# A linear-attention and SiLU MLP kernel: r and k turned on VectorE from a grouped copy, the product in four row groups, y and r16 turned by DMA, a ramp with half blocks

## The chip, the cores and the metric

The kernel runs on one core of a Trainium2 chip. The metric is the device time of one launch in microseconds (us). Before the change the median of two runs is 228.84 us (228.53 and 229.16). The profile is of one further execution of the same program.

## The reference

For four batches (B), eight heads (H), 768 tokens (S) and a head width D of 48, a decaying state is carried over the tokens, and its output goes through a two-layer MLP with SiLU.

```python
for t in range(S):
    cur = np.einsum('bhd,bhe->bhde', u[None] * kt, vt)
    y[:, :, t] = np.einsum('bhd,bhde->bhe', rt, state + cur)
    state = w[None, :, :, None] * state + np.einsum('bhd,bhe->bhde', kt, vt)
...
x = np.ascontiguousarray(attn_out.transpose(0, 2, 1, 3)).reshape(B * S, H * D)
h = x @ w_in
g = h * (1.0 / (1.0 + np.exp(-h)))
return (g @ w_out).astype(np.float32)
```

All inputs and the output are float32; x is 3072 x 384, w_in 384 x 2048, w_out 2048 x 384.

## The kernel before

The tokens are cut into six chunks of 128 (C). A unit is one chunk of one batch, so there are 24 units; unit i is chunk i // 4 of batch i % 4, and `sc` is the chunk. Each unit works on all eight heads, in four pairs (NP). One list of instructions is written out by hand for each engine: the kernel runs under a manual schedule, so each engine takes its work in the order of the program.

For one unit:

- `load` (L96 to L104) issues three DMAs on SP's queue for r, k and v, four units ahead (NIN is 4). A row of one head is 48 floats, so the pieces are 192 bytes long.
- `p1_natural` casts v to half precision on ScalarE and makes on GpSimd, from the rows as they lie, `ku` = k*u (L145), `rku_f` = r*ku (L147), and `kc`, k with the decay to the end of the chunk (L148). VectorE sums rku_f over a head (L151), and GpSimd makes `vu`, the bonus term (L153).
- `p1` turns r and k with eight TensorE transposes in float32 (L165) into PSUM. VectorE multiplies them by the decay tables into `rT` and `kT` (L167, L169). From chunk 1 on ScalarE casts rT to half precision (L172).
- `p2` multiplies kT by rT per head in float32: `ae` for the even heads in rows 0 to 47 (L179), `ao` for the odd ones in rows 64 to 111 (L181), each into a PSUM bank of its own. VectorE applies the causal mask to both (`am`, L186).
- `p3` adds up y in PSUM from the carried state and from am times v (L198, L201) and makes the new state's part `sps` (L208). VectorE adds vu to y (L211) and updates the state (L221, L224); GpSimd decays the state first (`sdec`, L215) and casts it afterwards (`stb`, L225).
- `p4` turns y with three TensorE transposes (L237), and ScalarE copies it into `xT` (L238), the input of the MLP for the whole chunk.

The MLP of a chunk is a list of 32 fillers. Sixteen are `l1`: three matmuls of 512 columns (L248) and one SiLU on ScalarE (L251). Sixteen are `l2`: four matmuls of 384 columns (L260), and after each fourth of these one eviction on VectorE (L264) and one store on SP (L266). The main loop puts eight fillers into each unit, in groups of two, one, two and three, between the steps of the unit. The four units of a chunk so take up the MLP of the chunk before. Units 0 to 3 have no fillers, and after unit 23 the 32 fillers of the last chunk are left.

The weights come through GpSimd's queue, w_in in three DMAs after unit 0's products (L285), w_out in four after unit 1's product (L292). PSUM is shared out as three banks for `tA` (tr, tk, ae, ao), two for `y` (y, sps, yT) and three for `moe` (hps, ops).

## Time and profile before

| | us |
|---|---|
| median of the runs | 228.84 |
| span of the profiled execution | 226.5 |
| first l1 matmul starts | 42.91 |
| unit 5 to unit 23, from one product to the next | 8.0 each |
| matmuls of the last chunk's MLP, after unit 23 | 20.8 |

| engine | busy us | share of the span |
|---|---|---|
| TensorE matmul | 202.3 | 89% |
| TensorE weight load | 133.1 | 59% |
| VectorE | 115.8 | 51% |
| ScalarE | 94.2 | 42% |
| GpSimd | 119.0 | 53% |

The span runs from the first to the last instruction of the profiled execution; the run's time has about 2.3 us more around it. A busy share is an average over a ramp, a long even stretch and a tail, so the stretches are read one by one. The busy times of two groups of matmuls can overlap, since matmuls are pipelined; the chain of waits counts each moment once.

### The profile page before, as it was taken

To read this page: it belongs to the slowest core of one execution; us is meant where nothing else is said; L and a number is where in the kernel's file an instruction comes from. 1 tells how busy PE (TensorE), PEld (TensorE's weight loads), DVE (VectorE), ACT (ScalarE), POOL (GpSimd) and SP (SyncE) were. 2 spreads that over 40 slices of the span, in tenths; PEclk is the share of its full clock that TensorE was granted. 3 is DMA by queue.
4 is the path that set the end of the run, shared out by engine and by line. 5 is a ranking of instruction groups with operands and counts; after the bars stand their busy time and mean duration, and the time that the engine had idled before them with its cause. 6 is when DMAs were issued, how large, how long until landed. Compare 5 with 4: busy or idle time off the path is not lost.

```text
span 226.5 us, 4378 instructions
## 1 busy us (share of the span) xinstructions
PE 202.3 (89%) x1672; PEld 133.1 (59%) x1672; DVE 115.8 (51%) x225; ACT 94.2 (42%) x173; POOL 119.0 (53%) x150
## 2 busy tenths in 40 slices
PE   1266298799999999999999999999999999999993
PEld 1164177456667656766665776666676557654561
DVE  6157365647368536656833865563685256420020
ACT  2521011586621378411578211866213783029500
POOL 2387975765674665667467466656746561000000
PEclk9999555799999999999999999999999999999999
DMA  5999999992216385026735053923161000110011
GB/s 95 201 196 208 204 185 176 224 186 50 58 38 139 105 177 104 3 76 137 166 77 107 0 142 98 213 48 61 38 142 69 3 0 3 69 53 16 3 69 69
DMA packets 81604, 22.69 MB, mean 100 GB/s; under 512 B 75824, under 2 KB 81200, under 8 KB 81584
## 3 DMA queue, kind: packets, MB, share of 16 engines
q1 hardware_dynamic: 79040, 19.28, 39.3%
q0 software_dynamic: 2544, 3.15, 8.0%
q8 instruction: 13, 0.21, 0.4%
q14 instruction: 7, 0.06, 0.1%
HBM read 20.84 MB, written 4.72 MB: 113 GB/s over the span
## 4 chain that ended last, share of the span: by engine, by line
PE 81%; POOL 8%; DVE 3%; issue 3%; DMA 2%; SPq 1%; DVEq 0%; POOLq 0%
PE hps L248 28%; PE ops L260 28%; PE ae L179 10%; PE tr L165 4%; PE tk L165 4%; PE yT L237 2%; DMA u_bc<-in_u_dram 2%; POOL ku L145 2%; PE y L201 2%; POOL rku_f L147 2%; PE sps L208 2%; PE y L198 2%; POOL wout L292 1%; SPq L102 1%; POOL kc L148 1%
## 5 line engine op out<-in xcount | busy, mean ns | idle before, releaser
L248 PE MATMUL hps<-xT,win 128*128 128x512 f16 x288 | 70.2, 384 | 0.0
L251 ACT ACTIVATE gT<-hps 128x512 f16<-128x512 f32 x96 | 57.4, 598 | 29.5 <-PE hps L248 27.3
L260 PE MATMUL ops<-wout,gT 128*128 128x384 f16 x384 | 69.0, 326 | 0.0
L260 PEld LDWEIGHTS <-gT 128*128 128x128 f16 x384 | 35.8, 98 | 21.2
L248 PEld LDWEIGHTS <-win 128*128 128x128 f16 x288 | 26.7, 99 | 26.5 <-issue 1.3
L186 DVE TENSOR_TENSOR am<-ae,maskM 128x512 f16<-128x512 f32 x24 | 16.6, 691 | 49.1 <-PE ao L181 49.1
L153 POOL TENSOR_TENSOR vu<-vin,rku 128x384 f32<-128x384 f32 x24 | 19.9, 829 | 35.8 <-DVE rku L151 35.8
L179 PE MATMUL ae<-rT,kT 48*128 48x128 f32 x192 | 30.8, 306 | 6.1 <-DVE kT L169 6.1
L179 PEld LDWEIGHTS ae<-rT,kT 48*128 48x128 f32 x192 | 25.8, 206 | 14.2 <-issue 7.5
L264 DVE COPY osb<-ops 128x384 f32<-128x384 f32 x24 | 13.4, 557 | 38.3 <-PE ops L260 37.9
L181 PE MATMUL ao<-rT,kT 48*128 48x128 f32 x192 | 30.8, 306 | 0.0
L238 ACT COPY xT<-yT 128x384 f16<-128x384 f16 x24 | 11.4, 476 | 43.3 <-PE yT L237 43.3
L145 POOL TENSOR_TENSOR ku<-kin,u_bc 128x384 f32<-128x384 f32 x24 | 24.1, 1005 | 7.9 <-DMA u_bc<-in_u_dram 6.7
L172 ACT CAST rT<-rT 112x512 f16<-112x512 f32 x20 | 12.4, 618 | 37.2 <-DVE rT L167 37.2
L181 PEld LDWEIGHTS ao<-rT,kT 48*128 48x128 f32 x192 | 25.8, 206 | 0.0
L147 POOL TENSOR_TENSOR rku_f<-rin,ku 128x384 f32<-128x384 f32 x24 | 24.0, 999 | 1.9
L148 POOL TENSOR_TENSOR kc<-kin,lamC 128x384 f16<-128x384 f32 x24 | 24.0, 999 | 0.8 <-ACT lamC L130 0.8
L225 POOL CAST stb<-st 112x384 f16<-112x384 f32 x20 | 10.1, 503 | 25.0 <-DVE st L221 19.9
L165 PE MATMUL tr<-ident,rin 128*112 128x128 f32 x96 | 16.7, 302 | 5.1 <-DMA rin<-in_r_dram 5.1
L167 DVE TENSOR_TENSOR rT<-tr,lamR 112x512 f32<-112x512 f32 x24 | 16.5, 689 | 4.2 <-PE tr L165 4.2
L151 DVE TENSOR_REDUCE rku<-rku_f 128x8 f32<-128x384 f32 x24 | 13.1, 544 | 10.2 <-POOL rku_f L147 10.1
L165 PEld LDWEIGHTS tr<-ident,rin 128*112 128x112 f32 x96 | 12.5, 147 | 9.0 <-issue 5.9
(46 smaller groups left out, 200.9 us busy)
## 6 DMA issues: line engine op xcount, KB each, us to landing
rin<-in_r_dram SPq DMA_DIRECT2D x24, 192.0 KB, 3.4
kin<-in_k_dram SPq DMA_DIRECT2D x24, 192.0 KB, 3.5
vin<-in_v_dram SPq DMA_DIRECT2D x24, 192.0 KB, 3.6
out_dram<-osb SPq DMA_DIRECT2D x24, 192.0 KB, 1.9
win<-in_moe_w_in_dram POOLq DMA_DIRECT2D x3, 512.0 KB, 8.8
wout<-in_moe_w_out_dram POOLq DMA_DIRECT2D x4, 384.0 KB, 10.3
w_bc<-in_w_dram SPq DMA_DIRECT2D x1, 192.0 KB, 4.3
u_bc<-in_u_dram SPq DMA_DIRECT2D x1, 192.0 KB, 4.1
```

The lines of the kernel that those rows point to most:

```text
L145: nc.gpsimd.tensor_tensor(out=ku, in0=kin[n][:, :, 0:D], in1=u_bc, op=ALU.mult)
L147: nc.gpsimd.tensor_tensor(out=rku_f, in0=rin[n][:, :, 0:D], in1=ku, op=ALU.mult)
L148: nc.gpsimd.tensor_tensor(out=kc[i % 2][:, :, 0:D], in0=kin[n][:, :, 0:D], in1=lamC, op=ALU.mult)
L153: nc.gpsimd.tensor_tensor(out=L["vu"], in0=vin[n], in1=rku.unsqueeze(2).broadcast_to([128, H, D]), op=ALU.mult)
L165: nc.tensor.transpose(t[0:PR, p, :], flat[:, 128 * p:128 * p + PR], ident)
L167: nc.vector.tensor_tensor(out=L["rT"], in0=tr[0:PR], in1=lamR, op=ALU.mult)
L179: nc.tensor.matmul(ae[:, p, :], L["kT"][0:D, p, :], L["rT"][0:D, p, :], start=True, stop=True)
L181: nc.tensor.matmul(ao[:, p, :], L["kT"][64:PR, p, :], L["rT"][64:PR, p, :], start=True, stop=True)
L186: nc.vector.tensor_tensor(out=am, in0=a, in1=maskM.unsqueeze(1).broadcast_to([128, NP, C]), op=ALU.mult)
L248: nc.tensor.matmul(hps, win[q][:, ft * 128:(ft + 1) * 128], xts[sc][:, q, :, :].rearrange("p b t -> p (b t)"), start=(q == 0), stop=(q == ...
L251: nc.scalar.activation(out=gts[sc][:, ft, :], in_=hps, func=AF.Silu)
L260: nc.tensor.matmul(ops, gts[sc][:, ft, b * C:(b + 1) * C], wout[:, ft, :], start=(ft == 0), stop=(ft == NFT - 1))
```

## The change

Units 0 to 3 keep TensorE for turning r, k and y. From unit 4 on:

- Four more DMAs per unit load r and k a second time in grouped form (`ldg`): partition 32*g + j holds four consecutive tokens of head pair g, in pieces of 768 bytes. `decay_g` multiplies them by decay tables in this layout on VectorE, into `rgd` and `kgd`, and `turn_g` turns them with two VectorE block transposes of 32 x 32, straight into SBUF.
- `product_g` does the product for all four head pairs at once in rows 0, 32, 64 and 96: three blocks of 32 rows with 256, 128 and 128 columns each, twelve matmuls in place of eight. Zeros between the two heads in rgd keep them apart.
- The half-precision r for the state comes from a GpSimd multiplication in natural layout (`decayed_r16`), turned by a DMA transpose on SP's queue (`turn_r16`); the ScalarE cast is gone.
- y is turned by a DMA transpose on SP's queue (`turn_y`), straight into xT; the TensorE transposes and the ScalarE copy are gone.
- l2's eviction goes from VectorE to ScalarE, but for the last chunk.

In the ramp, the small loads of w and u go on ScalarE's queue ahead of everything, the weights come in eight pieces spread over units 0 to 3, half of chunk 0's l1 (the first two batches, in matmuls of 256 columns) runs inside units 2 and 3, and the other half comes as eight fillers. PSUM becomes two buffers of two banks (`att`) and four banks (`moe`). Within a unit the fillers come in groups of two, two and four.

```diff
+    def ldg(i, dst, src):
+        sc, b = unit(i)
+        for h in range(2):
+            nc.sync.dma_start(
+                out=dst[i % NIN][:, h].rearrange("p a d -> p (a d)"),
+                in_=bass.AP(tensor=src.tensor, offset=(b * H + h) * S * D + sc * C * D,
+                            ap=[[2 * S * D, NP], [TB * D, TJ], [1, TB * D]]))
+
+    def load(i):
+        if i >= NU:
+            return
+        if i >= B:
+            ldg(i, rg, r)
+            ldg(i, kg, k)
+        ld(i, kin, k, 64)
+        ld(i, rin, r, 64)
+        ld(i, vin, v, D)
...
+    nc.scalar.preload_act_table_set("natural_log_exp_and_others")
+    nc.vector.memset(wpT, 1.0)
+    nc.scalar.dma_start(out=wpT[0:D, :], in_=bass.AP(tensor=w.tensor, offset=0,
+                                                     ap=[[1, D], [PW, NP]]))
+    nc.scalar.dma_start(out=wpT[64:PR, :], in_=bass.AP(tensor=w.tensor, offset=D,
+                                                       ap=[[1, D], [PW, NP]]))
+    nc.scalar.dma_start(out=u_bc, in_=bass.AP(tensor=u.tensor, offset=0,
+                                              ap=[[0, 128], [D, H], [1, D]]))
+    nc.scalar.dma_start(out=w_bc, in_=bass.AP(tensor=w.tensor, offset=0,
+                                              ap=[[0, 128], [1, HD]]))
+    nc.scalar.dma_start(out=w_g, in_=bass.AP(tensor=w.tensor, offset=0,
+                                             ap=[[PW, NP], [0, TJ], [1, PW]]))
...
+    def decay_pe(i):
+        for key, src, lam in (("rT", "tr", lamR), ("kT", "tk", lamK)):
+            L(i)[key] = wrk.tile([PR, NP, C], FP, name=key)
+            nc.vector.tensor_tensor(out=L(i)[key], in0=L(i)[src][0:PR], in1=lam, op=ALU.mult)
+
+    def product_pe(i):
+        a = L(i)["a"] = ps.tile([128, 2, NP, C], FP, name="a", tag="att", bufs=2)
+        rT, kT = L(i)["rT"], L(i)["kT"]
         for p in range(NP):
-            nc.tensor.matmul(ae[:, p, :], L["kT"][0:D, p, :], L["rT"][0:D, p, :],
-                             start=True, stop=True)
-            nc.tensor.matmul(ao[:, p, :], L["kT"][64:PR, p, :], L["rT"][64:PR, p, :],
-                             start=True, stop=True)
-        L["am"] = []
-        for a in (ae, ao):
-            am = wrk.tile([128, NP, C], F16, name="am", bufs=4)
-            nc.vector.tensor_tensor(out=am, in0=a,
-                                    in1=maskM.unsqueeze(1).broadcast_to([128, NP, C]),
-                                    op=ALU.mult)
-            L["am"].append(am)
-
-    def p3(i):
-        sc, b = unit(i)
-        L = live[i]
-        v16 = L["v16"]
-        y = ps.tile([128, H, D], FP, tag="y", bufs=2)
+            for j, r0 in ((0, 0), (1, 64)):
+                nc.tensor.matmul(a[:, j, p, :], kT[r0:r0 + D, p, :], rT[r0:r0 + D, p, :],
+                                 start=True, stop=True)
+
+    def decay_g(i):
+        n = i % NIN
+        d = L(i)["rgd"] = rgd[i % 2]
+        nc.vector.tensor_tensor(
+            out=bass.AP(tensor=d.tensor, offset=d.offset,
+                        ap=[d.ap[0], [H1, 2], [128, TB], [1, D]]),
+            in0=rg[n], in1=lamRG, op=ALU.mult)
+        kd = L(i)["kgd"] = wrk.tile([128, TB, 2, D], FP, name="kgd")
+        nc.vector.tensor_tensor(out=kd.rearrange("p a h d -> p h a d"), in0=kg[n],
+                                in1=lamKG, op=ALU.mult)
+
+    def decayed_r16(i):
+        nc.gpsimd.tensor_tensor(out=r16[i % 2][:, :, 0:D], in0=rin[i % NIN][:, :, 0:D],
+                                in1=lamRn, op=ALU.mult)
+
+    def turn_r16(i):
+        L(i)["rT16"] = wrk.tile([128, NP, C], F16, name="rT16")
+        nc.sync.dma_start_transpose(out=L(i)["rT16"],
+                                    in_=r16[i % 2].rearrange("p h d -> p (h d)"))
+
+    def turn_g(i):
+        rT = L(i)["rT"] = wrk.tile([128, 4, C], FP, name="rTg")
+        kT = L(i)["kT"] = wrk.tile([128, 3, C], FP, name="kTg")
+        nc.vector.transpose(
+            out=kT.rearrange("p b (j a) -> p a b j", a=TB),
+            in_=L(i)["kgd"].rearrange("p a h d -> p a (h d)").rearrange("p a (b j) -> p a b j", j=TJ))
+        nc.vector.transpose(
+            out=rT.rearrange("p b (j a) -> p a b j", a=TB),
+            in_=L(i)["rgd"].rearrange("p a (b j) -> p a b j", j=TJ))
+
+    def product_g(i):
+        a = L(i)["ag"] = [ps.tile([128, 2, 512], FP, name="ag", tag="att", bufs=2) for _ in range(2)]
+        rT, kT = L(i)["rT"], L(i)["kT"]
+        for blk, r0, n, c0 in ((1, 1, 2, 0), (0, 0, 1, 0), (2, 3, 1, 128)):
+            for g in range(NP):
+                rows = slice(TJ * g, TJ * g + TJ)
+                nc.tensor.matmul(a[g // 2][:, g % 2, c0:c0 + 128 * n],
+                                 kT[rows, blk, :],
+                                 rT[rows, r0:r0 + n, :].rearrange("p b t -> p (b t)"),
+                                 start=(blk == 1), stop=(blk != 1), skip_group_check=True)
...
+        ys = L(i)["ys"] = ps.tile([128, 2, 512], FP, name="ys", tag="att", bufs=2)
+        y = ys[:, 0, 0:HD].rearrange("p (h d) -> p h d", h=H)
...
+    def turn_y(i, by_pe):
+        sc, b = unit(i)
+        yf = L(i)["y16"].rearrange("p h d -> p (h d)")
+        x = x_tile(sc)
+        if not by_pe:
+            nc.sync.dma_start_transpose(out=x[:, :, b, :], in_=yf)
+            return
...
+        m = B // nb
+        hps = ps.tile([128, m, nb * C], FP, name="hps", tag="moe", bufs=4)
+        for f in range(m):
+            for q in range(NQ):
+                nc.tensor.matmul(hps[:, f, :], win[:, q, (ft + f) * 128:(ft + f + 1) * 128],
+                                 xts[sc][:, q, b0:b0 + nb, :].rearrange("p b t -> p (b t)"),
+                                 start=(q == 0), stop=(q == NQ - 1))
+        nc.scalar.activation(out=gts[sc][:, ft:ft + m, b0 * C:(b0 + nb) * C], in_=hps, func=AF.Silu)
...
+            if sc < NCH - 1:
+                nc.scalar.copy(out=osb, in_=ops)
+            else:
+                nc.vector.tensor_copy(out=osb, in_=ops)
...
+    def second(sc):
+        return [lambda b=b, p=p: l2(sc, b, p) for b in range(B) for p in range(4)]
+
+    def first(sc):
+        return [lambda f=f: l1(sc, 0, B, f) for f in range(NFT)]
+
+
+    bonus_products(0)
+    ld_win(0)
+    decayed_k(0)
+    turn_pe(0)
+    decay_pe(0)
+    cast_v(0)
+    tables_g()
+    for i in range(2):
+        nc.vector.memset(kc[i][:, :, D:64], 0.0)
+        nc.vector.memset(rgd[i][:, :, D:H1], 0.0)
+        nc.vector.memset(r16[i][:, :, D:64], 0.0)
+    for b in range(B):
+        nc.gpsimd.memset(st[b], 0.0)
+    for i in range(B):
+        product_pe(i)
+        bonus_sum(i)
+        masked(i)
+        bonus_v(i)
+        if i == 0:
+            ld_win(1)
+        if i == 1:
+            ld_win(3)
+        if i == 2:
+            ld_wout(1)
+        if i + 1 < B:
+            bonus_products(i + 1)
+            if i == 0:
+                ld_win(2)
+            if i == 1:
+                ld_wout(0)
+            turn_pe(i + 1)
+        if i == 2:
+            for ft in range(0, NFT // 2, 2):
+                l1(0, 0, 2, ft)
+        if i == 3:
+            for ft in range(NFT // 2, NFT, 2):
+                l1(0, 0, 2, ft)
+        outputs(i)
+        if i + 1 < B:
+            decay_pe(i + 1)
+        evict_y(i)
+        state(i)
+        load(i + NIN)
+        if i + 1 < B:
+            decayed_k(i + 1)
+            cast_v(i + 1)
+        turn_y(i, True)
+        if i == 2:
+            ld_wout(2)
+        if i == 3:
+            ld_wout(3)
+    fillers.extend([lambda ft=ft: l1(0, 2, 2, ft) for ft in range(0, NFT, 2)])
+    fillers.extend(second(0))
+
+    def prepare(i):
+        bonus_products(i)
+        decayed_k(i)
+        decay_g(i)
+        decayed_r16(i)
+        turn_r16(i)
+
+    prepare(B)
+    turn_g(B)
+    cast_v(B)
+    bonus_sum(B)
+    bonus_v(B)
+    decayed_state(B)
+    for i in range(B, NU):
+        sc, b = unit(i)
+        product_g(i)
+        masked(i)
+        if i + 1 < NU:
+            prepare(i + 1)
         fill(2)
-        if i == 1:
-            for g in range(4):
-                nc.gpsimd.dma_start(
-                    out=wout[:, 4 * g:4 * g + 4, :],
-                    in_=moe_w_out[512 * g:512 * g + 512, :]
-                    .rearrange("(f p) n -> p f n", p=128))
+        outputs(i)
+        evict_y(i)
+        state(i)
+        turn_y(i, False)
+        load(i + NIN)
+        fill(2)
         if i + 1 < NU:
-            p1_natural(i + 1)
-            p1(i + 1)
-        load(i + NIN)
-        fill(1)
-        p3(i)
-        fill(2)
-        p4(i)
-        fill(3)
-        sc, b = unit(i)
+            turn_g(i + 1)
+            cast_v(i + 1)
+            bonus_sum(i + 1)
+            bonus_v(i + 1)
+            decayed_state(i + 1)
+        fill(4)
         if b == B - 1:
-            fill(len(fillers))
-            fillers.extend(moe(sc))
+            fillers.extend(first(sc) + second(sc))
```

## The prediction

> **What bounds the kernel now.** I read the page's busy times, then its slices, then the chain of waits over one unit in the even stretch, then the groups of instructions for what the other engines carry. In the slices each digit is tenths of a fortieth of the span (5.7 us); PEclk is TensorE's granted clock and DMA the share of the DMA engines.
>
> ```profile
> PE 202.3 (89%) x1672; PEld 133.1 (59%) x1672; DVE 115.8 (51%) x225; ACT 94.2 (42%) x173; POOL 119.0 (53%) x150
> ...
> PE   1266298799999999999999999999999999999993
> ...
> PEclk9999555799999999999999999999999999999999
> DMA  5999999992216385026735053923161000110011
> ```
>
> The 89% splits in two. In the first eight slices TensorE has gaps, in four of them half its clock, and the DMA engines are full from the second to the ninth. After that TensorE never rests, and DMA averages 0.45 over 76 to 108 us. One unit of that stretch in the chain (start, length, what):
>
> ```profile
> 115.40 0.30 PE ae L179
> ...
> 116.49 1.40 PE hps L248 x6
> 117.89 0.44 PE tr L165 x4
> 118.33 0.44 PE tk L165 x4
> 118.77 0.65 PE hps L248 x3
> ...
> 119.80 0.23 PE sps L208 x4
> 120.02 1.29 PE hps L248 x6
> 121.32 0.17 PE yT L237 x3
> 121.49 1.94 PE hps L248 x9
> 123.43 0.30 PE ae L179
> ```
>
> From ae to ae is 8.03 us, all TensorE: the eight fillers take 5.28 (1.40 + 0.65 + 1.29 + 1.94), the product 1.09 (115.40 to 116.49), the turns of r and k 0.88, that of y 0.17, y and sps 0.61. So a unit's own TensorE work is 2.75. What other engines do costs nothing until one of them needs about 8 us per unit. GpSimd is nearest:
>
> ```profile
> L145 POOL TENSOR_TENSOR ku<-kin,u_bc 128x384 f32<-128x384 f32 x24 | 24.1, 1005 | 7.9 <-DMA u_bc<-in_u_dram 6.7
> L147 POOL TENSOR_TENSOR rku_f<-rin,ku 128x384 f32<-128x384 f32 x24 | 24.0, 999 | 1.9
> L148 POOL TENSOR_TENSOR kc<-kin,lamC 128x384 f16<-128x384 f32 x24 | 24.0, 999 | 0.8 <-ACT lamC L130 0.8
> L153 POOL TENSOR_TENSOR vu<-vin,rku 128x384 f32<-128x384 f32 x24 | 19.9, 829 | 35.8 <-DVE rku L151 35.8
> ```
>
> Mean lengths in ns stand after the busy time. With sdec (0.83) and stb (0.50) GpSimd has 5.16 us of work per unit, and waits for VectorE in the rest.
>
> **What the Trainium skill says.** "TensorE: Matmul & The Clock Gate", in "Why this matters for your kernels", has matmuls of few rows run side by side when they start at partitions 0, 32, 64 and 96: four of them 3.07 times as fast as in turn. The trace before has two such groups: ae and ao start within 10 ns of each other, and a pair of passes takes 0.11 us. Four are not in it. "VectorE: DVE Perf Modes", in "The three transpose paths", gives 311 ns for a 128 x 128 transpose in blocks of 32 on VectorE and 1309 ns on the DMA crossbar, both in half precision; no run here shows either. "SBUF — State Buffer", in "Who interferes with whom", says that a VectorE instruction with two SBUF inputs and a GpSimd instruction that reads SBUF block each other entirely. In the even stretch VectorE's two-input work takes one input from PSUM, so the trace shows no such clash; decay_g will have two SBUF inputs.
>
> **The change, part by part, for units 4 to 23.**
>
> *TensorE.* Turns of r and k go (0.88), and of y (0.17). The product keeps its streaming time if four groups overlap: 256 + 128 + 128 columns are as many as the four pairs of 128 before. But each 0.11 us must then take four weight loads instead of two. Lower bound 1.05 us; upper bound for the theory 1.6; I take 1.2. Own work becomes 2.75 - 0.88 - 0.17 + 0.11 = 1.81, a unit 7.1 us.
>
> *VectorE.* The PSUM multiplications (0.69 + 0.68) and osb (0.56 in half of the units) go. decay_g adds two instructions of 384 elements; as y's addition of that size, 0.56 each (0.5 at least, since no VectorE row of 384 elements is under 0.54; 1.0 if a GpSimd instruction blocks it). turn_g adds transposes of 384 and 512 elements. Their nearest rows are the reduce over 384 (0.54) and the mask over 512 (0.69): 1.25 together; half of that if two elements pass per cycle, 2.5 if four-byte elements take two passes. With masks 1.37, y 0.56, state 0.71 and the reduce 0.54 that is 5.55 us, under 7.1. The loop back to TensorE is longer: product 1.2, handover 0.1, masks 1.37, decay_g 1.1, y 0.56, state 0.71, turn_g 1.25, handover 0.1, so 6.4. It leaves 0.7.
>
> *GpSimd.* decayed_r16 is another kc: 1.0 (0.83 at least). 6.16 us per unit, 0.9 under the period. decay_g lies beside these instructions; blocked, it costs GpSimd up to 1.1 and VectorE a wait of about half an instruction twice. That eats both slacks: 0 to 0.5 us per unit, taken as 0.1.
>
> *SP's queue and DMA.* Per unit SP issued three loads (0.37 + 0.52 + 0.65 at 86 us) and a store (about 0.6). Four grouped loads at 0.4 make 3.7, and two transposes come on top. The order is turn_r16(i+1), turn_y(i), loads; turn_r16 waits for GpSimd at about 5.5 us into the unit, and holds up turn_y, the loads and stores behind it. The loads are four units ahead, and the stores have three buffers, so this costs nothing there. DMA time per unit was 0.45 of 8.03, so 3.6; 512 pieces of 768 bytes add 0.6 by count, 2.3 by bytes, say 1.1. For the transposes, 224 KB per unit, "DMA: Bandwidth & Descriptors" has 261 GB/s in "Latency and other measured facts": 0.9 us, an estimate from that page. At 5.6 of 7.1 DMA doesn't bind. Nor does ScalarE: it loses 0.62 and 0.48 per unit and gains 0.56.
>
> *PSUM.* y and sps share a buffer with the product, so the next product waits for y's addition and the state. Six fillers (3.9 us) hide these 1.3 us. In unit 7 that cover is gone: chunk 0 leaves only 24 fillers for 32 places. Its chain is product 1.2, masks 1.5, outputs 0.6, y's addition behind decay_g, turn_y behind turn_r16, until the next l1 at about 8.5 to 9 us, where TensorE has about 3 us of work. I take 5.5 lost (3 to 8). At the ends of chunks 2, 3 and 4 turn_y lands about 0.5 late each: 1.5.
>
> *Ramp.* Before, unit 4's product starts at 41.5. GpSimd started at 9.14, when u_bc landed; on its own queue it lands at about 7. From there GpSimd's row of work for units 0 to 3 is four times about 5.8 (products 2.0, kc 1.0, vu 0.83, stb 0.5, two weight issues of 0.6 to 0.78), the memsets of the state (1.6 on VectorE before, say 2), then unit 4's four products: 37, and VectorE's turn puts unit 4's product at 38. DMA binds alike: units 0 to 3 and w_in must pass first (13.8 + 9 at the full rate, then unit 4's 4.7 beside w_out). Range 33 to 43. Half of chunk 0's l1, 5.2 us, is done by then.
>
> **The sum.** In the profiled execution 185.0 us follow unit 4's product: 20 units at 2.75 (55, less 0.9 for the last four without sps), 6 chunks of MLP at 20.77 (124.6), 3.7 of last store, and 2.6 for the slow clock after 41.5. Afterwards: 20 x 1.81 - 0.9 = 35.3, plus 124.6 - 5.2 = 119.4, plus 3.7 and 2.6: 161.0. With the ramp 38, unit 7 5.5, chunk ends 1.5 and blocking 2 the span is 208.0. The median shown is 2.3 above the span before, so 210.3: **210 us**.
>
> **The rivals.**
>
> 1. *The DMA transposes are slow.* At 1309 ns for each 128 x 128 block, seven per unit are 9.2 us on SP's queue or the crossbar; with 3.7 of other issues a unit is 12.9 instead of 7.1: 38 + 20 x 12.9 + 20.8 + 3.7 + 2.3 = 323. It decides once the two take over about 4.3 us (8.0 less 3.7), slower than before from about 4.8. For it: no row shows one. Against: that page's price may be mostly latency, which runs beside other work. 0.16.
> 2. *GpSimd becomes the bound* through blocking: 6.16 + 1.1, and VectorE's waits of about 0.6 in the same loop: 7.9 per unit, 20 x 0.7 more than the 0.1 taken: 224. For it: slack of only 0.9. 0.16.
> 3. *Four row groups overlap only in pairs:* product 1.9, 224; in turn 3.6, 258. The two groups seen speak against the latter. 0.08.
> 4. *The change does less than it says:* units 0 to 3 keep TensorE's turns and full DMA engines, so the ramp may gain nothing. Alone that is 215, within the first case.
>
> **How the numbers follow.** The forecast has 0.60; its own range is 196 (product 1.05, ramp 33, unit 7 3, no blocking) to 226 (ramp 43, product 1.5, unit 7 8). About 2% is what a measurement of this kernel tells from no change, so faster means below 224.3. Most of the first case lies there and half of the second and third: 0.67. Within 2%, the rest of the second mostly: 0.13. Slower, the first rival and the tail of the others: 0.20. The range of 196 to 232 takes in rivals 2 to 4 and leaves out the first and groups wholly in turn.
>
> **What would show it.** Products about 7.1 us apart in chunks 2 to 5; ag's twelve matmuls in about 1.2; ku still near 1.0 beside decay_g; the crossbar transposes landing within 3 us and SP idle part of each unit; one gap of 4 to 8 us at unit 7; unit 4's product at 33 to 43. If SP's queue or a wait of outputs for rT16 leads the waits, rival 1 is right; if kc or vu stretch and VectorE waits for GpSimd, rival 2; starts of ag's row groups 0.1 us apart, rival 3.

## The result: 277 us, where 210 was forecast

| | before | after |
|---|---|---|
| median of the runs (lowest to highest), us | 228.84 (228.53 to 229.16) | 277.46 (276.41 to 278.50) |
| span of the profiled execution, us | 226.5 | 274.7 |
| unit 4's product starts at, us | 41.4 | 36.8 |
| unit 4's product to unit 5's, us | 9.7 | 33.3 |
| unit 4's product to unit 23's, mean step, us | 8.09 | 10.88 |
| unit 23's product to the end, us | 31.4 | 31.2 |

The ratio is 1.216 (1.198 to 1.234): 21.6% slower. Of the 48.2 us between the spans, the start of unit 4's product gives back 4.6 and the tail 0.2. All of the loss, 53 us, lies in the 19 steps from unit 4's product to unit 23's. The list of their starts splits it: the step from unit 4 to 5 costs 23.6 more than before. Four more steps (8 to 9, 12 to 13, 16 to 17 and 20 to 21: 15.8, 14.7, 11.9 and 14.4 us) cost 24.8 more than four of 8.0. The other fourteen cost some 5 more in all. So within a chunk most steps are 6.8 to 8.3 us, near the 7.1 of the forecast (three are 9.7 to 10.9), and once per chunk TensorE stops.

First the same parts of the page as before the change: busy times, then TensorE, its clock and the DMA engines in fortieths of the span (6.9 us each).

```profile
PE 194.2 (71%) x1660; PEld 119.0 (43%) x1660; DVE 147.9 (54%) x235; ACT 86.4 (31%) x164; POOL 149.9 (55%) x180
...
PE   2578760008995349897479777868986378999994
...
PEclk9999977555999658999959979879999869999999
DMA  6999995663746655645746647756644746132011
```

TensorE fell from 89% to 71%. It has a hole in the seventh to ninth slice, and a dip at each chunk's end. The granted clock falls where the holes are, and the work just behind one runs slower too: six matmuls of l1 take 2.72 us behind a hole of 5.1 us at 99.8, and 1.47 us at 109.5. No engine is near full, and the DMA engines are mostly at 4 to 7 tenths: nothing on this page is the bound. The chain of waits doesn't help, since it breaks off before the even stretch. So I went to the list of waits (engine and line, what was waited for, total us, times, longest):

```profile
PEld L305 <- DMA rT<-r: 37.9, 9, 22.4
...
PE ys L305 <- DMA rT<-r: 32.3, 8, 22.0
...
PE hps L375 <- DMA xT<-y: 20.0, 4, 5.8
```

Those are the two transposes by DMA. The longest wait, 22 us, is unit 4's: `outputs` needs rT16. The question is whether the transfer is slow or starts late. The timeline of SP's queue (start, length, what) around that wait:

```profile
58.08 2.01 SPq L74 DMA_DIRECT2D vin<-in_v_dram  x1
60.20 2.61 SPq L256 DMA_TRANSPOSE rT<-r  x2
```

and TensorE's line that ends the wait:

```profile
63.09 0.26 PE L305 MATMUL ys<-stb,rT 112*128 112x96 f16 x1 [22.04 <-DMA rT<-r]
```

GpSimd had finished r16 for unit 4 at 41.2 us. SP, however, was busy from 19.3 to 60.1 with the loads of units 4 to 7. It issued the transpose at 60.20, and `outputs` started 2.9 us later. The transfer isn't slow: **it starts 19 us late, because of what stands before it in SP's queue**.

The same queue in the even stretch of after, one round:

```profile
146.12 1.25 SPq L256 DMA_TRANSPOSE rT<-r  x1
147.46 1.20 SPq L359 DMA_TRANSPOSE xT<-y  x1
148.71 1.17 SPq L81 DMA_DIRECT2D rg<-in_r_dram  x2
149.93 1.11 SPq L81 DMA_DIRECT2D kg<-in_k_dram  x2
151.08 0.48 SPq L74 DMA_DIRECT2D kin<-in_k_dram  x1
151.60 2.64 SPq L74 DMA_DIRECT2D rin<-in_r_dram  x1
154.28 1.96 SPq L74 DMA_DIRECT2D vin<-in_v_dram  x1
156.35 1.25 SPq L256 DMA_TRANSPOSE rT<-r  x1
```

and of the kernel before:

```profile
86.25 0.37 SPq L102 DMA_DIRECT2D rin<-in_r_dram  x1
86.72 0.52 SPq L102 DMA_DIRECT2D kin<-in_k_dram  x1
87.35 0.65 SPq L102 DMA_DIRECT2D vin<-in_v_dram  x1
```

From transpose to transpose is 10.2 us, and SP is issuing in nearly all of it. The page's busy times have no row for SP. Added up from the timeline, the issues that start from 100 to 180 us take 74.8 of these 80 us, against 20.3 before. The rest is gaps of 0.04 to 0.11 us between one issue and the next, 5.0 us together: SP never rests, and so never waits for GpSimd's r16 there. The products agree: from unit 5 to unit 21, four units take 38.4 to 41.3 us, 9.9 per unit. In means of the issues from 100 to 180, one unit's are:

| issue | after | e1_g16 (below) | before |
|---|---|---|---|
| r and k grouped | 4 of 0.55 = 2.2 | 8 of 0.50 = 4.0 | none |
| kin, rin, vin | 0.48, 1.95, 2.06 | 0.43, 0.58, 0.67 | 0.63, 0.46, 0.76 |
| transposes of r16 and y | 1.24 + 1.22 | 1.34 + 1.23 | none |
| store | 0.5 | 0.5 | 0.4 |
| sum | 9.6 | 8.7 | 2.2 |

Two things stand out: each transpose takes 1.2 us of issue, and rin's and vin's issue are 1.4 us longer than before, though these two lines weren't changed. They stand behind the grouped loads, so the grouped loads' own transfer is suspect. At 42 to 44 us VectorE waits for rg, and next to nothing but the grouped pieces of 768 bytes moves. The windows (us, busy time of each engine with its number of instructions, TensorE's clock, DMA share, GB/s) of that moment and of the even stretch:

```profile
42.00:44.00 2.00, 0.00 (x0) 0.00 (x0) 0.18 (x1) 0.00 (x0) 0.80 (x2) 1.00 0.27 90
100.00:180.00 80.00, 64.21 (x544) 35.95 (x542) 52.37 (x80) 25.18 (x48) 51.27 (x56) 0.88 0.61 137
```

0.27 of 16 DMA engines is 4.3. The Trainium skill has the reason in "DMA: Bandwidth & Descriptors", under "Why a DMA increments its semaphore by 16 and not by 1": a DMA runs on the largest number of engines, up to 16, that divides the slowest dimension (of more than 1) on both sides. `ldg` reads DRAM with `[2*S*D, NP]` ahead, a dimension of 4. The trace names no engines, but it has the packets one by one: from 42 to 44 us never fewer than four are under way at once, and exactly four for two thirds of the time. That agrees with the page.

### The profile page after: what moved, and what is told of

It is laid out like the page before. It is cut to its first block, busy times and chain, and to the rows that moved or that the text cites. A ratio compares the mean times of both kernels' runs of the same rounds, so it can differ in the third digit from the quotient of the medians.

```text
span 274.7 us, 4456 instructions
## 1 busy us (share of the span) xinstructions
PE 194.2 (71%) x1660; PEld 119.0 (43%) x1660; DVE 147.9 (54%) x235; ACT 86.4 (31%) x164; POOL 149.9 (55%) x180
## 5 line engine op out<-in xcount | busy, mean ns | idle before, releaser
L375 PE MATMUL hps<-xT,win 128*128 128x512 f16 (+1 forms) x336 | 75.8, 386 | 20.0 <-DMA xT<-y 20.0
L291 DVE TENSOR_TENSOR am<-ag,maskM 128x512 f16<-128x512 f32 x40 | 25.8, 685 | 34.6 <-PE ag L275 34.6
L210 POOL TENSOR_TENSOR vu<-vin,rku 128x384 f32<-128x384 f32 x24 | 19.9, 830 | 38.3 <-DVE rku L205 34.1
L330 DVE TENSOR_TENSOR y<-ys,vu 128x384 f16<-128x384 f32 x24 | 13.3, 552 | 46.8 <-issue 24.0
L275 PE MATMUL ag<-rTg,kTg 32*128 32x128 f32 (+1 forms) x480 | 24.7, 336 | 10.6 <-DVE rTg L265 10.6
L197 POOL TENSOR_TENSOR rku_f<-rin,ku 128x384 f32<-128x384 f32 x24 | 26.2, 1091 | 3.9 <-DMA rin<-in_r_dram 2.0
L275 PEld LDWEIGHTS ag<-rTg,kTg 32*128 32x128 f32 x480 | 20.4, 195 | 18.0 <-issue 8.2
L200 POOL TENSOR_TENSOR kc<-kin,lamC 128x384 f16<-128x384 f32 x24 | 27.7, 1156 | 0.1
L247 DVE TENSOR_TENSOR kgd<-kg,lamKG 128x384 f32<-128x384 f32 x20 | 24.8, 1239 | 2.2 <-DMA kg<-in_k_dram 2.2
L251 POOL TENSOR_TENSOR r<-rin,lamRn 128x384 f16<-128x384 f32 x20 | 22.8, 1138 | 0.0
L265 DVE STREAM_TRANSPOSE rTg<-rgd 128x512 f32<-128x512 f32 x20 | 21.6, 1078 | 0.0
L242 DVE TENSOR_TENSOR rgd<-rg,lamRG 128x384 f32<-128x384 f32 x20 | 16.8, 841 | 2.7 <-DMA rg<-in_r_dram 2.7
L262 DVE STREAM_TRANSPOSE kTg<-kgd 128x384 f32<-128x384 f32 x20 | 17.6, 878 | 0.5
```

The costliest lines, as they stand in the source:

```text
L197: nc.gpsimd.tensor_tensor(out=L(i)["rku_f"], in0=rin[n][:, :, 0:D], in1=ku, op=ALU.mult)
L200: nc.gpsimd.tensor_tensor(out=kc[i % 2][:, :, 0:D], in0=kin[i % NIN][:, :, 0:D], in1=lamC, op=ALU.mult)
L210: nc.gpsimd.tensor_tensor(out=L(i)["vu"], in0=vin[i % NIN], in1=L(i)["rku"].unsqueeze(2).broadcast_to([128, H, D]), op=ALU.mult)
L247: nc.vector.tensor_tensor(out=kd.rearrange("p a h d -> p h a d"), in0=kg[n], in1=lamKG, op=ALU.mult)
L251: nc.gpsimd.tensor_tensor(out=r16[i % 2][:, :, 0:D], in0=rin[i % NIN][:, :, 0:D], in1=lamRn, op=ALU.mult)
L265: nc.vector.transpose(out=rT.rearrange("p b (j a) -> p a b j", a=TB), in_=L(i)["rgd"].rearrange("p a (b j) -> p a b j", j=TJ))
```

## The experiments

The expectations name theories by letters. A is that the grouped loads' few engines hold SP's queue; B that the plain length of SP's issues binds; C that the DMA transposes are the cause, whatever the loads do. Numbers in each table row: median, ratio with its interval, unit 4's product, step 4 to 5, mean step from unit 4 to unit 23, and the length of SP's issues that start in the 80 us from 100 to 180.

| kernel | us | ratio | unit 4 at | 4 to 5 | step | SP |
|---|---|---|---|---|---|---|
| before | 228.84 | | 41.4 | 9.7 | 8.09 | 20.3 |
| after | 277.46 | 1.216 (1.198 to 1.234) | 36.8 | 33.3 | 10.88 | 74.8 |
| e1_g16 | 260.90 | 1.141 (1.127 to 1.156) | 36.1 | 27.4 | 10.17 | 72.9 |
| e2_g_on_act | 267.24 | 1.169 (1.166 to 1.173) | 52.6 | 19.7 | 9.55 | 55.6 |
| e3_pe_turns | 238.78 | 1.045 (1.034 to 1.055) | 42.5 | 11.0 | 8.64 | 72.6 |
| e4_no_grouped | 229.09 | 0.998 (0.994 to 1.003) | 42.9 | 10.5 | 8.10 | 53.0 |
| e5_g16_pe_turns | 228.33 | 1.002 (0.999 to 1.006) | 41.9 | 9.6 | 8.10 | 57.4 |
| e7_before_plus_g4 | 238.35 | 1.049 (1.037 to 1.060) | 44.5 | 11.0 | 8.49 | 73.1 |
| e8_before_plus_g16 | 229.77 | 1.011 (1.000 to 1.022) | 41.9 | 10.6 | 8.13 | 59.1 |
| e14_r16_on_pe | 257.50 | 1.123 (1.116 to 1.131) | 38.3 | 11.9 | 9.77 | 74.5 |
| e15_y_on_pe | 263.22 | 1.148 (1.136 to 1.161) | 39.7 | 30.2 | 9.96 | 71.9 |

**Grouped loads on more engines (e1).** The same bytes, cut by head pair, so that a DMA's slowest dimension is 32 and not 4. This takes eight DMAs instead of four.

```diff
-        for h in range(2):
-            nc.sync.dma_start(
-                out=dst[i % NIN][:, h].rearrange("p a d -> p (a d)"),
-                in_=bass.AP(tensor=src.tensor, offset=(b * H + h) * S * D + sc * C * D,
-                            ap=[[2 * S * D, NP], [TB * D, TJ], [1, TB * D]]))
+        for g in range(NP):
+            (eng or nc.sync).dma_start(
+                out=dst[i % NIN][TJ * g:TJ * g + TJ].rearrange("p h a d -> p h (a d)"),
+                in_=bass.AP(tensor=src.tensor, offset=(b * H + 2 * g) * S * D + sc * C * D,
+                            ap=[[TB * D, TJ], [S * D, 2], [1, TB * D]]))
```

> The grouped loads are made per head pair, eight DMAs of 32 partitions instead of four of 128, so that the slowest dimension of both sides is 32 and not 4. Theory A (the four DMAs each run on only four of the sixteen DMA engines, 128 pieces of 38 ns, 4.9 us per unit, and with the other packets these four carry about 9.5 us per unit, which holds SP's queue up): the r and v loads' issues fall from 2 to 0.6 us, SP's loop becomes about 9.1 us by issues alone, total about 250. Theory B (SP's queue is bound by the plain length of its issues): four issues of 0.55 us more per unit, 12.1 us per unit, total about 319. Theory C (the DMA transposes are the cause, whatever the loads do): no change, 277.

The timeline of SP's queue in e1:

```profile
153.96 1.37 SPq L256 DMA_TRANSPOSE rT<-r  x1
155.42 1.47 SPq L359 DMA_TRANSPOSE xT<-y  x1
156.95 1.98 SPq L81 DMA_DIRECT2D rg<-in_r_dram  x4
158.97 1.83 SPq L81 DMA_DIRECT2D kg<-in_k_dram  x4
160.85 0.43 SPq L74 DMA_DIRECT2D kin<-in_k_dram  x1
161.32 0.58 SPq L74 DMA_DIRECT2D rin<-in_r_dram  x1
162.00 0.67 SPq L74 DMA_DIRECT2D vin<-in_v_dram  x1
```

rin's issue falls from 1.95 to 0.58 and vin's from 2.06 to 0.67, without an edit to either: they had been held by the grouped loads ahead of them. That part of A stands. The kernel still takes 261, since four more issues eat most of what rin and vin gave back, and the queue's sum stays at 8.7. With the gaps between its fourteen or so issues, 0.9 us per unit, that is the step of 9.6 us from unit 9 to unit 21: SP doesn't rest in e1 either.

**Grouped loads on ScalarE's queue (e2).** `nc.sync` becomes `nc.scalar` in `ldg`, nothing else.

> The four grouped loads of a unit are issued from ScalarE's queue instead of SP's, with the same pieces. Theory A (four engines carry 9.5 us per unit): the same engines have the same work, so units stay at about 9.5 us, total 265 to 277. Theory B (length of SP's issues): SP's loop falls by 2.3 us to 7.6 us, total about 230. Theory C (transposes): no change, 277.

SP's issues fall to 55.6 of 80, and the time is still 267, as A had it. But A isn't shown by that, since the edit brings a loss of its own: ScalarE can stand still between one grouped load and the next (e9, below, shows how). In the ramp two of them are issued 4.5 us apart ahead of v's cast, TensorE waits 8.3 us for that cast, and unit 4's product starts at 52.6 instead of 36.8. The run shows that ScalarE's queue is no cure as this program uses it, not what SP's queue alone costs.

**Both transposes on TensorE (e3).** r16 and y are turned by matmul, r16's two fillers before a unit's end and y's behind the unit's fourth filler, and ScalarE copies them out.

```diff
-        nc.sync.dma_start_transpose(out=L(i)["rT16"],
-                                    in_=r16[i % 2].rearrange("p h d -> p (h d)"))
+        t = ps.tile([128, NP, C], F16, name="r16T", tag="moe", bufs=4)
+        rf = r16[i % 2].rearrange("p h d -> p (h d)")
+        for p in range(NP):
+            nc.tensor.transpose(t[:, p, :], rf[:, 128 * p:128 * p + 128], ident16)
+        nc.scalar.copy(out=L(i)["rT16"], in_=t)
...
-        turn_y(i, False)
...
+        turn_y(i, True)
...
```

> y and r16 are turned by TensorE and copied by ScalarE in units 4 to 23 too; no DMA transposes. The grouped loads stay. Theory A: the four engines keep 8.4 of 9.5 us per unit, total about 245 to 250. Theory B: SP's loop falls by 2.45 us to 7.4 us, TensorE needs 7.4 us, total about 222. Theory C: as B, about 222, with the wait of 22 us in unit 4 gone.

239: below what A says and above what its rivals say. Neither cause alone carries the loss. SP still doesn't rest: from unit 9 to 21 a step is 8.4 us, 7.7 of issues and 0.7 of gaps. What now comes late are the stores. At 120 us TensorE waits 3.3 us for ScalarE, and ScalarE 7.1 us for a store that stands in SP's queue.

**Grouped loads left out (e4).** rg and kg stay zero, so the product within the chunk is missing from the output; every instruction but the loads remains, and eight memsets on VectorE write the zeros.

> This kernel leaves the grouped loads out (the grouped rows are zeros, written once), so the product within a chunk is left out of the output's value, but every instruction on the compute engines and both DMA transposes stay. Theory A: DMA engines and SP (about 5.2 us per unit) are free, TensorE bounds, total about 215, as forecast for the whole change. Theory B: SP's loop about 5.2 to 7.6 us, total about 215 to 230. Theory C (transposes): 265 to 277.

The 22 us wait is gone (step 4 to 5 is 10.5), and SP rests for some 3 us per unit, but 229 is not the 215 expected. A part of that is the run's own: its memsets hold VectorE from 13.3 to 16.6 us, and unit 4's product starts 6.1 us later than in after. The other part is the step, 7.6 us within a chunk. The chain of waits of e4 (start, length, engine, what, line) says why:

```profile
133.59 1.16 PE ag L272 x24
134.75 1.31 PE ops L384 x8
136.07 0.80 DVE rgd L239
136.87 1.27 DVE kgd L244
138.14 0.47 DVE y L327
138.61 0.26 DVE st L338
...
138.88 0.37 DVE st L338
...
139.28 0.88 DVE kTg L259
140.15 0.92 DVE rTg L262
```

This is the forecast's loop of product, masks, decay_g, y, state and turn_g. The masks take 1.29 us beside the eight ops, which the chain names. The loop was forecast at 6.4 and is 7.6: kgd takes 1.27 instead of 0.56 and rgd 0.80, the two transposes 1.80 instead of 1.25. It leads the period here, and TensorE waits for rTg. So the forecast had a second error, which the first had covered.

**Both edits (e5).** e1's loads with e3's turns.

> Both of the edits that helped alone: grouped loads over sixteen engines, and y and r16 turned by TensorE, so SP issues eight grouped loads, three loads and a store, about 6.0 us per unit. If SP's queue was the bound of the changed kernel, units fall to the loop through VectorE (product 1.16, masks 1.3, decay_g 2.15, y 0.47, state 0.63, turn_g 1.8: 7.6 us as in the run without grouped loads), total 222 to 226. If the DMA engines themselves (mean share 0.5 to 0.6) were the bound, the gains don't add up and it stays at 235 or above.

228.3, a little above the range expected. With e1 and e3 it completes a table of the two causes:

| | four-engine loads | loads by head pair |
|---|---|---|
| transposes by DMA | 277.5 (after) | 260.9 (e1) |
| transposes on TensorE | 238.8 (e3) | 228.3 (e5) |

The transposes by DMA cost 39 or 33 us, net of what the turns cost on TensorE, and the four-engine loads 17 or 10. Both together are 49.1 us. That after is slower than before by nearly the same, 48.6, is chance: e5 has the change's shorter TensorE work and VectorE's longer loop, and at 41.4 us TensorE has waited 5.7 us for GpSimd's r16, whose turn stands ahead of unit 4's product in e5.

It is no single slow operation, but a queue that is overfilled by both. From unit 9's product to unit 19's, SP has no gap over 0.42 us in after, e1, e3, e14 and e15, while TensorE waits; in e5 it rests 0.8 us per unit, and the chunk ends cost next to nothing more (steps of 7.8 to 8.3 us from unit 9 on). A rival would be that the DMA engines are short of bandwidth. Against it, their mean share from 100 to 180 us is 0.61 in after and 0.65 in e10 (below), which does a unit in 7.3 us.

**The loads alone, in the kernel before (e7, e8).** The kernel before plus unused grouped loads, in the change's form (e7) or in e1's (e8). Nothing reads them, so only queue and DMA time are added.

```diff
         sc, b = unit(i)
+        if i >= B:
+            ldg(i, rg, r)
+            ldg(i, kg, k)
         for t, src, wd in ((rin, r, 64), (kin, k, 64), (vin, v, D)):
```

> The kernel before with the four grouped loads of a unit added on SP's queue and used by nobody. Theory A (four of sixteen engines, 4.9 us more on them per unit): they carry 8.4 us per unit, over the 8.0 of before, and the ramp, whose DMA engines are full, loses more: 238 to 250. If only the length of SP's issues counts (3.7 + 2.3 = 6.0 us, under 8.0), no change in the even stretch: 229 to 231.

> The same bytes added to the kernel before, but in eight DMAs that run on all sixteen engines. Theory A: 1.2 us more per engine and unit, 4.8 of 8.0 us, so the even stretch is unchanged and the ramp loses 2 to 4 us: 229 to 233, clearly under the one with four engines. If only the length of SP's issues counts: more issues, so not under it.

e8 costs about 1% (its interval begins at 1.000), with steps of 8.0. In e7 the even steps remain at 8.0 us too: of the 10.8 us between its span (237.3) and that of before, 3.1 lie ahead of unit 4, 1.3 in step 4 to 5 and 6.4 in one step, 8 to 9, of 14.4. So the four-engine loads do keep up with 8.0 us, and my 8.4 was too high. The queue is busy for 73.1 of 80 us even so, 7.3 per unit, and its longest gap is 0.44 us. That is a queue which is just not overfull: SP hardly rests, and TensorE is busy for all of the 80 us. Two transposes of 1.2 on top make an estimate of 9.8 of issues per unit; after has 9.3 in a step of 9.9.

**One transpose at a time (e14, e15).** e14 turns r16 on TensorE and leaves y on the DMA; e15 the reverse.

> The changed kernel with r16 alone turned by TensorE and copied by ScalarE; y stays on the DMA transpose behind it. If r16's place on SP's queue (waiting for GpSimd, ahead of y and the loads) holds the rest up, the step from unit 4 to 5 and the chunk ends both shrink: 240 to 250, near the 238.8 of both turns moved. If each transpose counts by its 1.2 us of issue, half of the 38 us between 277 and 239 comes back: 256 to 260.

> The changed kernel with y alone turned by TensorE; r16 stays on the DMA transpose. The waits at the chunk ends for xT go, but outputs still waits for r16 through SP's queue, whose work falls only to about 8.7 us per unit, and the step of 33 us stays: 258 to 270. If y's turn was the costly one, 240 to 250.

Both came out as expected. Their gains, 20.0 and 14.2 us, make 34.2 of e3's 38.7. Away from the ramp (units 9 to 21) a step takes 10.03 us in after, and 9.26 and 9.24 with one transpose less: either is worth 0.8 us per unit there, of 1.24 and 1.22 us of issue; the queue still fills with the loads that are held (rT's own issue is 1.39 in e15). So the transposes cost most of their issue time, whichever of them it is. The wait for rT16 alone wasn't the cause: e14 has no transpose for it and still ends its chunks with steps of 13 to 15 us. Its step 7 to 8 is even 19.4: TensorE waits 13.0 us for ScalarE's copy of rT16, and ScalarE up to 17.1 us for a store behind the loads on SP.

**Order instead of quantity (e12, e13).** e13 puts the loads of units 6 and 7 behind the transposes of units 4 and 5. e12 fetches all loads two units ahead instead of four.

```diff
-        load(i + NIN)
+        if i < 2:
+            load(i + NIN)
...
+        if i == B:
+            load(B + 2)
+            load(B + 3)
         load(i + NIN)
```

> The changed kernel, but on SP's queue the loads of units 6 and 7 stand behind unit 4's and 5's transposes instead of ahead of them; loads stay four units ahead from there on. If the wait of 22 us in unit 4 is a matter of that order alone, the step from unit 4 to 5 falls from 33 to about 14 us and the total to 252 to 258. If SP's queue is bound by its whole work (about 9.9 us per unit from the ramp to the last load), the wait only moves to the next units: the step falls, units 5 to 8 get longer, total 266 to 277.

> The changed kernel with loads issued two units ahead instead of four, so that in the ramp the loads of units 6 and 7 no longer stand ahead of unit 4's r16 on SP's queue. If the wait of 22 us in unit 4 comes from that order, the step from unit 4 to unit 5 falls from 33 to 12 to 16 us and the total to 255 to 262; the gaps at the chunk ends stay, since SP's work per unit is the same. If the wait is the transpose's own travel, 277.

In e13 (282.46 us, 1.232) step 4 to 5 falls from 33.3 to 16.0, but step 6 to 7 rises to 21.6: the wait only moves, and the total is above both ranges of its expectation. In either order the queue was short of the same time. e12 (345.02 us, 1.509) fell short of its aim, because every unit then waits for its own loads, GpSimd for kin 157 us in all. It says nothing on the order.

**DMA transposes kept, the loads over two queues (e9).** e1's loads, with k's on ScalarE's queue.

> As the kernel with grouped loads over sixteen engines and both DMA transposes kept (260.9 us), but the grouped loads of k are issued on ScalarE's queue. Pieces, engines and transposes are the same. If SP's queue was the bound (about 9.3 us of issues per unit, now about 7.1), units fall to VectorE's loop of 7.6 us and the gaps at the chunk ends shrink: 232 to 242. If the DMA engines or the transposes' own travel were the bound: 258 to 265.

250.11 us (1.093), a miss: SP has 62.9 of 80 and rests for 1.7 us per unit, but now ScalarE is held. Its timeline, and below it the lengths (ns: shortest, median, longest) of the single issues:

```profile
125.36 5.49 ACTq L81 DMA_DIRECT2D kg<-in_k_dram  x4
130.90 1.09 ACT L378 ACTIVATE gT<-hps 128x512 f16<-128x512 f32 x2 [5.00 <-DMA out_dram<-osb]
```

```profile
L81 ACTq DMA_DIRECT2D kg<-in_k_dram x80: 317/383/1029, 19.9 to 189.5; - x80
```

The 5.49 us run from the start of the first issue to the end of the fourth, and the issues themselves take 0.3 to 0.55 us each, no more than on SP. The rest are pauses between them, of 2.9 us before the third and 1.0 us before the fourth. Each of these two starts 0.02 us after an update of the semaphore that it waits for. It is one of eight that the program's DMAs of both queues use in turn, so an issue waits until the DMA that had the semaphore last has landed. On SP such waits don't show, as its gaps in after and e1 are too short; on ScalarE they hold up the activations and copies behind the loads.

**Towards a faster version (e6, e10, e11).** All three start from e5, and their edits are shown against it. e6 runs decay_g and turn_g two units ahead, to take them out of VectorE's loop.

> As the kernel with both edits, but decay_g and turn_g are done two units ahead, behind the state, so that the next product no longer waits for them. If the loop through VectorE bounds at 7.6 us, units fall to what VectorE and TensorE need by themselves, 7.2 to 7.4 us: 4 to 8 us less than without it, total 215 to 220. If VectorE's own work or GpSimd bounds instead (GpSimd has 6.2 us and is blocked by decay_g), no gain, 222 to 226.

233.38 us (1.025 (1.016 to 1.035)), slower than e5. In the profiled execution (236.24 us) steps alternate between 7.3 and 9.3 us. Two waits of e6 say why:

```profile
POOL vu L210 <- DVE rku L205: 38.1, 19, 5.4
PEld L259 <- POOL r L251: 25.2, 11, 5.9
```

VectorE makes the turns ahead of the sum rku, so vu on GpSimd waits for it, r16 behind vu, and TensorE, in order, for r16. e10 moves the sum ahead of the turns, r16's turn just behind the product, and y's turn behind three fillers.

```diff
         product_g(i)
+        turn_r16(i)
         masked(i)
...
-        fill(2)
+        fill(3)
         turn_y(i, True)
         if i + 1 < NU:
-            turn_g(i + 1)
-            cast_v(i + 1)
             bonus_sum(i + 1)
+        for n in ([i + 1] if i < B + 2 else [i + 1, i + 2] if i == B + 2 else [i + 2]):
+            if n < NU:
+                decay_g(n)
+                turn_g(n)
...
```

> TensorE turns and sixteen engines as before, decay_g and turn_g two units ahead, but now the sum for vu comes ahead of them on VectorE, r16 is turned one unit later (right after its unit's product) and y one filler later. If the miss of the first two-ahead version came from TensorE waiting for GpSimd's r16 and GpSimd for VectorE's sum, units are even at 7.3 to 7.5 us, total 216 to 222. If GpSimd and VectorE are the bound by their own work under blocking, 7.8 us and 226 to 232.

221.52 us, 0.963 (0.956 to 0.971). The window of its even stretch (columns as above):

```profile
100.00:180.00 80.00, 80.00 (x816) 49.31 (x814) 69.58 (x107) 45.56 (x89) 70.11 (x75) 1.00 0.65 150
```

TensorE is busy for 80.00 of 80 us at full clock and a unit takes 7.3: TensorE is the bound again. SP's queue is nearly full here too, with 6.4 us of issues and 0.9 of gaps per unit. e11 also puts decay_g's table for k into PSUM, so that VectorE reads one input from SBUF and not two; the MLP's PSUM buffers become three instead of four.

```diff
-    lamKG = cst.tile([128, 2, TB, D], FP)
+    lam_ps = ps.tile([128, 512], FP, name="lam_ps", tag="lam", bufs=1)
+    lamKG = lam_ps[:, 0:HD].rearrange("p (h a d) -> p h a d", h=2, a=TB)
...
```

> As the reordered kernel, with the decay table of k kept in PSUM (three buffers instead of four for the MLP), so that kgd has one SBUF input. If decay_g and GpSimd block each other over the second SBUF input, kgd falls from 1.2 to 0.56 us, and GpSimd's kc, rku_f or r beside it fall back to 1.0; total equal to the reordered kernel or up to 6 us less. If kgd is long for its layout, it stays at 1.2.

Groups by shape: e10's and, below it, e11's line for the same operation.

```profile
L247 DVE TENSOR_TENSOR kgd<-kg,lamKG 128x384 f32<-128x384 f32 x20 | 24.4, 1219 | 0.0
```

```profile
L248 DVE TENSOR_TENSOR kgd<-kg,lam_ps 128x384 f32<-128x384 f32 x20 | 11.1, 553 | 0.5
```

From 1219 to 553 ns by the table's place, with the same shapes and layout. GpSimd gains too: ku goes from 1.06 to 1.005 us and sdec from 1.10 to 0.82. The whole is 219.32 us, 0.957 (0.950 to 0.964), the fastest kernel of the study. Against e10 the gain of 2.2 us is less sure, as the even steps are 7.3 in both. These versions keep the change's row-group product, VectorE turns and half-block ramp; what they give up is the turning by DMA and the four-engine form of the loads.

## Why the prediction was wrong

**The step that failed is "SP's queue and DMA".** It added SP's issues to 3.7 us, wrote that "two transposes come on top", and put no number on them: the only price they got was 0.9 us of DMA travel. Their travel is cheap, as forecast. One unit's 896 packets of 256 bytes at 21 ns make 1.2 us of all 16 engines, and in e9 y's transposes land 2.5 us after issue in the median (2.3 to 3.5, between 100 and 135 us). What counts is the issue: 1.24 + 1.22 us on a queue in which everything is in order. The second gap in that step is the grouped loads, taken as 4 x 0.4 us of issue, with their 1.1 us of DMA time spread over all engines. On about four, the two loads behind them hold SP for 2.8 us more (1.95 + 2.06 against 0.58 + 0.67 in e1). The sum was to be 3.7 and a little, and is 9.6. The step ends with "this costs nothing there", said of the loads and stores that come late. It didn't ask what stands behind the loads: rT16 and xT are wanted at once, and wait for them. Nor does it hold for the stores, in spite of their three buffers: ScalarE waits 21.0 us for them in after, four times.

**The ramp's price came from the same queue.** The ramp's sum covered GpSimd and DMA time up to unit 4's product (38 forecast, 36.8 measured). The number is right in part by luck: GpSimd ends its four products for unit 4 at 41.2 us and not at 37, and the product didn't wait for them, since it needs only VectorE's turn of rg and kg behind unit 3's y. The sum didn't follow SP's queue to the transpose behind the sixteen grouped loads of units 4 to 7. That is the 23.6 us.

**Rival 1 named the place, and not the size.** SP's issues did pass 8.0 us per unit, and its sign came, "a wait of outputs for rT16 leads the waits" (of TensorE's waits it is the longest). But it wanted over 4.3 us from the two transposes, priced them at 9.2, and 2.46 were measured; it had 323 us where it was 277. The rest of the load on SP came from the grouped loads, which neither the rival nor the forecast had.

**VectorE's loop was mis-sized by 1.2 us.** Forecast 6.4, in e4 7.6. These are the terms of the change on VectorE and GpSimd, groups by shape in after:

```profile
L247 DVE TENSOR_TENSOR kgd<-kg,lamKG 128x384 f32<-128x384 f32 x20 | 24.8, 1239 | 2.2 <-DMA kg<-in_k_dram 2.2
...
L265 DVE STREAM_TRANSPOSE rTg<-rgd 128x512 f32<-128x512 f32 x20 | 21.6, 1078 | 0.0
L262 DVE STREAM_TRANSPOSE kTg<-kgd 128x384 f32<-128x384 f32 x20 | 17.6, 878 | 0.5
L242 DVE TENSOR_TENSOR rgd<-rg,lamRG 128x384 f32<-128x384 f32 x20 | 16.8, 841 | 2.7 <-DMA rg<-in_r_dram 2.7
```

```profile
L200 POOL TENSOR_TENSOR kc<-kin,lamC 128x384 f16<-128x384 f32 x24 | 27.7, 1156 | 0.1
L197 POOL TENSOR_TENSOR rku_f<-rin,ku 128x384 f32<-128x384 f32 x24 | 26.2, 1091 | 3.9 <-DMA rin<-in_r_dram 2.0
...
L251 POOL TENSOR_TENSOR r<-rin,lamRn 128x384 f16<-128x384 f32 x20 | 22.8, 1138 | 0.0
```

turn_g is 1.96 us (1.25 taken, 2.5 the upper bound), decay_g 2.08 (1.1 taken, 2.0 if blocked). Behind the bar stand busy us and mean ns: rku_f rose from 999 to 1091 and kc from 999 to 1156 beside them. That is the mutual blocking which the Trainium skill states in "SBUF — State Buffer", "Who interferes with whom"; e11 agrees, with kgd at 553 ns and kc at 1002. I had taken 0.1 us per unit for it, and within the loop it is about 1. Rival 2 had this blocking and put 7.9 us per unit, and e4 and e5 show 7.6 and 7.8. Its number is near, but it made GpSimd the bound, and e4's chain runs through VectorE.

**What held.** The four row groups run side by side: 24 passes in 1.09 to 1.16 us (1.2 forecast), so rival 3 is out. TensorE's period was forecast at 7.1 with the turns gone; e10, which has them back on TensorE at 0.33 + 0.17 us, runs at 7.3, so the forecast was 0.3 too high here. The gap at unit 7 came, but larger. From its product to the next l1 it is 14.8 us (8.5 to 9 forecast), of which TensorE is idle for 10.8 (5.5 forecast, 3 to 8), 5.1 of it the wait for xT; in e4 it is 11.2 and 7.0, in e5 9.3 and 4.3. The other chunk ends cost 4 to 7 us each where 0.5 was forecast, through the same queue. Two readings were loose, and little rests on them: three slices of the page before stand at half the clock, the fourth at 7 tenths; and a run's time is 1.7 to 1.8 us above its own span, not 2.3.

**Not settled.** What lets a load's issue end once the grouped loads ahead of it have moved isn't in the trace; that they hold it is shown by e1. The clock that TensorE is granted falls behind each hole (mean 0.88 in the window of after, 1.00 in e10's); how much of the loss it makes wasn't separated from the waits. The steps of 13.5 and 8.8 us behind unit 4's product in e10 were not followed up. No run has the transposes or the stores on another queue with the loads kept on SP.

## What to carry to other kernels

Add up the issue time of every DMA queue per unit of work, as for an engine, with the gaps between issues, since the page's busy times leave it out: here 2.2 us became 9.6, where 8.0 was the period before. A transfer that is wanted at once shouldn't stand in order behind prefetches that are not; where the queue was full, re-ordering only moved the wait (e13). And look at the slowest dimension of a new access pattern before its bytes are priced: e1 moves the same bytes and saves 17 us.

## What the runs showed of the hardware

- A transpose by DMA of 128 x 512 or 128 x 384 half-precision elements takes 1.2 us of SP's queue to issue (medians 1.24 and 1.20 in after, up to 2.19 and 1.36); before, a plain load takes 0.46 to 0.76 in the mean.
- A load's issue grew from 0.58 to 1.95 us and from 0.67 to 2.06 by what stood ahead of it in the queue, without an edit to it (e1 and after).
- Loads whose DRAM side begins with a dimension of 4 kept four packets under way at once, and never fewer, while little else moved (after, 42 to 44 us).
- A transpose in blocks of 32 on VectorE, in fp32, takes 0.88 us for 128 x 384 and 1.08 us for 128 x 512.
- A VectorE multiplication of 128 x 384 with both inputs in SBUF takes 0.54 us at its shortest and 1.35 in the median beside GpSimd's work (kgd in after); with one input in PSUM 0.543 to 0.556 (e11).
